# Six pairs of hidden blocks, in two groups of three, take seven products in GEMM2; a convolution's two filters come ahead of v; four row tiles load by halves

## The chip, the cores and the metric

The kernel runs on one core of a Trainium2 chip. The metric is the device time of one execution in microseconds (us). TensorE (PE) multiplies, VectorE (DVE) and ScalarE (ACT) do elementwise work, GpSimd (POOL) and SyncE (SP) issue the transfers (DMAs); each engine works through its own instructions in order.

## The reference

```
xn  = layernorm(x)                                  # x: 2048 x 1024
h   = silu(xn @ w1)                                 # w1: 1024 x 3584
ffn = h @ w2                                        # w2: 3584 x 1024
kv  = shift(k) * v                                  # 4 taps along the sequence, per channel
y   = irfft(rfft(pad kv) * rfft(pad ssm_k)) + kv * ssm_D
out = x + xn * y + ffn
```

The shapes are S = 2048 rows, D = 1024 channels and F = 3584 hidden columns, all float32.

## The kernel before, in words

**Numbers.** Every float32 operand of a matrix product is split into two float16 parts, hi and lo (`split`: ScalarE writes hi = scale x source, VectorE writes lo = the rest). A product of two operands is three matmuls: hi x hi, hi x lo, lo x hi.

**The two GEMMs.** GEMM1 makes the 28 hidden blocks of 128 columns, two by two (14 pairs), for all 16 row tiles of 128 rows. Of the 28 combinations of a pair and a half of the rows, 26 go through `units`, a seven-product (Strassen-like) form: of a 2 x 2 product of blocks it makes seven products P1 to P7 instead of eight, with sums of blocks as factors. GEMM2 multiplies the hidden blocks by w2, whose 1024 result columns fall into two halves of W = 512.

GEMM2 has two parts. The *plain* part takes the blocks that are not in `PAIRS` (`PLAIN`, 20 of 28) in `NC` = 5 chunks of four, for each half of the columns h and each row tile t: twelve matmuls per chunk (`steps2`, L1128 to L1130), summed in one PSUM bank over the chunks, and written out by `result`. The *seven-product* part (`units2`) takes the blocks of the four pairs of `PAIRS`. It has eight units; one is a 2 x 2 product of two row tiles (`tiles2`) by the two halves of the columns. A unit makes P1, P7, P6, P2, P5, P3, P4, each of twelve matmuls (four pairs x three). Products share banks: P6, P5 and P3 are added onto a copy of P1 in a second bank, so each of them waits until `evacuate2` has copied the bank's last state away (`seen`), and P4 is added onto P7's bank. Four results per unit are scaled and added to `out` in memory. The factors for this form are made beforehand: `quad` makes the seven sums of the hidden blocks during GEMM1 and stores them (`hsf`), and `norms_w2` makes the seven factors of w2 and keeps them in the eight large buffers `places`.

**The convolution.** `convolution` runs beside both GEMMs, on 8 groups g of 128 channels. Per group: `gate` (four taps and the product with v, on ScalarE and VectorE), `signal_parts` (hi and lo parts), `stage1` (matmuls of a long transform, L1630 to L1632, whose banks `to_spec` empties with ScalarE and VectorE), `transforms` (forward, spectrum product and inverse, all on VectorE), `result_parts` and `stage1_inv` (matmuls back, L1818 to L1820), `gated` (product with xn, and the write to `out`). `stage1` of group g can empty its banks only when the parts of group g - 1 are taken. It has the two PSUM banks of `ps_r`; the inverse and small norms have the two of `py_r`; the feed-forward part has four (`ff`), of which one may be lent when `spare()` says so: between GEMM1's end and the last part.

**What sets the order.** A planner on the host (`Order`) holds many streams of steps; it gives each step a cost, picks the step that can start first (with a small bias per stream) and emits it to its engine. So the order on each engine is fixed before the run, and an engine that waits holds up all behind it. `flag[...]` tokens order the streams among themselves; on the chip, semaphores follow the data.

**Writes to `out`.** Three contributions meet in each element: plain part, seven-product part, convolution. `L` is a plain transfer from SP, `G` an adding transfer from POOL. The plain part's first half of columns and the convolution's first four groups store with `L`; the others add with `G` and wait for the flags `row` or `conv row`. The very last unit waits for `conv out`, all writes of the convolution, before it goes on past P6: it then loads the tile of `out`, adds to it, and stores with `L`.

**The start.** `load_row` loads a row tile of x (128 x 1024, 512 KB) in one transfer; VectorE takes the statistics of each half of it (L546). Until the first row tiles are normalised, transposed and split, TensorE runs filler matmuls (L1896, L1903).

Of the kernel before, what the change touches and what calls it, by code (L numbers as in the profile page):

```python
# [20 lines left out]
P = 128  # L21
# [4 lines left out]
NT = S // P  # L26
# [27 lines left out]
PAIRS = (8, 9, 10, 11)  # L54
UNITS = [[*range(2, NP)], [NP - 1, 0, 1, *range(2, NP - 1)]]
NQ = len(PAIRS)
# [246 lines left out]
def h3_ffn_kernel(ctx, tc, x, kp, vs, fs, shift, dskip, w1, w2, cfwd, cinv, out):  # L303
# [77 lines left out]
    hsf = [{p[0]: dram.tile([4, P, NQ, 2, P], F16, name=f"hsf{p[0]}{b}") for p in PRODUCTS.values()} for b in range(2)]  # L381
# [474 lines left out]
    def quad(i, sp):  # L856

        def factors(names, hf, toks=()):
# [4 lines left out]
            for f, name in enumerate(names):  # L863
                yield L(hsf[sp][name][:, :, PAIRS.index(i)].rearrange("q p h s -> p q (h s)"),
                        ht[:, 4 * f:4 * f + 4].rearrange("p q h s -> p q (h s)"))
                ttok.set()
# [18 lines left out]
    for sp in range(2):  # L885
        flag["quads", sp] = Token(NQ)

# [197 lines left out]
    def feed_forward():  # L1085
# [13 lines left out]
        for h in range(2):  # L1099
            for ts in TOGETHER[h]:  # L1100
                pos = {}
                for c in range(NC):
                    for t in ts:
                        if c == 0:
                            yield ff.ready
                            pos[t] = ff.tile([P, W])
                        yield flag["h", h, t, c]
                        hx, htok = flag["h", h, t, c].what
                        yield flag["w2", h, c]
                        wc, wtok = w2c[h, c]  # L1110
                        yield from steps2(pos[t][0], hx, wc, c == 0, c == NC - 1)
                        htok.set()
                        if t == NT - 1:
                            wtok.set()
                        if c == NC - 1:
                            add(result(h, t, *pos[t]), EB)
        flag["last part"].set()
        yield from units2()


    TOGETHER = ([range(3)] + [(t,) for t in range(3, NT)],
                [(t,) for t in range(NT - 3)] + [range(NT - 3, NT)])

    def steps2(po, hx, wc, first, last, more=False):
        for n in range(4):
            def mm(n=n):
# [3 lines left out]
                nc.tensor.matmul(po, hx[:, n, 1, :], wc[:, n, 0, :], start=False, stop=last and n == 3, **kw)  # L1130
# [15 lines left out]
    def units2():  # L1146

        def product2(n, u, o, first=False, cols=slice(0, W), end=True):
            yield flag["h2", u, n]
            hx, htok = flag["h2", u, n].what  # L1150
            yield flag["w2f", n]
            wc, wtok = w2f[n]
            yield from steps2(o[:, cols], hx, wc[:, :, :, cols], first, True, not first)
# [5 lines left out]
        def start(u):  # L1159
# [4 lines left out]
            add(evacuate2(u, one, made, seen), EB)  # L1164
# [3 lines left out]
        for u in range(len(tiles2)):  # L1168
# [23 lines left out]
            if u + 1 < len(tiles2):  # L1192
                following = yield from start(u + 1)
# [4 lines left out]
            if u + 1 < len(tiles2):  # L1198
# [6 lines left out]

    def at(u, r, h):

        sp, q = tiles2[u]
        t = 4 * (2 * sp + r) + q
        return orr[t // T2, t % T2, :, h * W:(h + 1) * W]  # L1210

    def evacuate2(u, one, made, seen):

        last = u == len(tiles2) - 1
# [5 lines left out]
        def copied(src, tok, to):  # L1220
# [3 lines left out]
            yield G(to, o)  # L1224
# [16 lines left out]
        if not last:  # L1241
            yield made["P2"]
            add(copied(*one, at(u, 0, 0)), EB)
# [7 lines left out]
        if last:  # L1251
            yield made["P2"]
            add(copied(*one, at(u, 0, 0)), EB)
        yield G(at(u, 1, 1), d)
# [5 lines left out]
        add(copied(two, k2, at(u, 0, 1)), EB)  # L1260
        if not last:
# [3 lines left out]
            yield G(at(u, 1, 0), a)  # L1265
# [11 lines left out]
    for n in range(NT):  # L1277
        flag["conv row", n] = Token(NG // 2)

    def columns(h):  # L1280

        return slice((1 - h) * W, (2 - h) * W)

    def result(h, t, po, tok):
# [4 lines left out]
        to = orr[t // T2, t % T2, :, columns(h)]  # L1289
        if h == 0:  # L1290
            yield L(to, o)
            flag["row", t].set()
        else:
            yield flag["conv row", t]
            yield G(to, o)
        otok.set()

    def load_h():
        yield flag["factors"]
        for h in range(2):  # L1300
            for c, t in [(c, t) for ts in TOGETHER[h] for c in range(NC) for t in ts]:
# [4 lines left out]
        for u, n in uses2():  # L1306
            sp, q = tiles2[u]
            yield wo.ready
            flag["h2", u, n].what = o, _ = wo.tile([P, NQ, 2, P], F16)
            yield L(o, hsf[sp][PRODUCTS[n][0]][q])  # L1310
            flag["h2", u, n].set()
# [20 lines left out]
    def norms_w2():  # L1332
# [17 lines left out]
        add(load_w2(), 0.05)  # L1350
        for h in range(2):
            for c in range(NC):
                r = places[W2PLACE[h][c]]
                yield r.ready
                if (h, c) == (0, 0):
                    yield flag["x", 1, "A22"]
                wc, wtok = w2c[h, c] = r.tile([P, 4, 2, W], F16)
                flag["w2", h, c].n = 2
                for a in (0, 2):
                    i = PLAIN[4 * c + a] // 2  # L1360
                    raw, tok = yield from next_w2()
# [607 lines left out]
```

## Time and profile before

| what | value |
|---|---|
| three runs | 1238.85, 1239.23, 1240.17 us; median 1239.23 |
| the profiled execution, its own time | 1239.78 us |
| its span, first to last instruction | 1237.8 us |
| granted TensorE clock | 0.999 |
| first and last GEMM1 matmul of L985 | 15.6 and 574.8 us |
| first and last GEMM2 matmul of L1128 | 576.7 and 1232.4 us |
| first and last matmul of the transform, L1630 | 278.5 and 1135.9 us |
| data moved | 278.77 MB, 225 GB/s on the mean |

Times in the page and the views are microseconds from the span's start, unless marked ns. A row of a group of instructions reads: line, engine, operation, out<-in by the program's names, shapes, count | busy us, mean ns of one | idle time of the engine just before them, and what ended it. A row of a window reads: from:to, length, then for each engine its busy time and its instructions, the granted clock, the share of time in which the DMA engines were busy, and GB/s. A row of the timeline reads: start, duration, engine, line, operation, out<-in, count, and in brackets the idle time before it and what ended it. A row of the waits reads: who <- for whom: us in total, times, longest.

### The profile page before, as it was taken

To read this page: it belongs to the slowest core of one execution; us is meant where nothing else is said; L and a number is where in the kernel's file an instruction comes from. 1 tells how busy PE (TensorE), PEld (TensorE's weight loads), DVE (VectorE), ACT (ScalarE), POOL (GpSimd) and SP (SyncE) were. 2 spreads that over 40 slices of the span, in tenths; PEclk is the share of its full clock that TensorE was granted. 3 is DMA by queue.
4 is the path that set the end of the run, shared out by engine and by line. 5 is a ranking of instruction groups with operands and counts; after the bars stand their busy time and mean duration, and the time that the engine had idled before them with its cause. 6 is when DMAs were issued, how large, how long until landed. Compare 5 with 4: busy or idle time off the path is not lost.

```text
span 1237.8 us, 16864 instructions
## 1 busy us (share of the span) xinstructions
PE 1227.2 (99%) x6044; PEld 597.6 (48%) x6044; DVE 1106.9 (89%) x1248; ACT 775.0 (63%) x1357; POOL 83.3 (7%) x93
## 2 busy tenths in 40 slices
PE   9999999999999999999999999999999999999998
PEld 8544444444444544445444544544454454444444
DVE  7999996996999779998999899799889979997992
ACT  7868897886687877659643832734363365536243
POOL 0000000000000000000000000001030130113114
PEclk9999999999999999999999999999999999999999
DMA  9598989899799889989876556489586775877767
GB/s 368 128 315 271 318 298 327 264 255 214 252 320 293 235 270 273 312 231 321 297 245 175 154 183 172 135 280 275 129 177 169 168 162 153 190 160 128 156 134 102
DMA packets 277700, 278.77 MB, mean 225 GB/s; under 512 B 85616, under 2 KB 204656, under 8 KB 276336
## 3 DMA queue, kind: packets, MB, share of 16 engines
q1 hardware_dynamic: 261888, 261.17, 70.0%
q0 software_dynamic: 15728, 16.52, 10.3%
q8 instruction: 47, 0.77, 0.3%
q14 instruction: 37, 0.30, 0.1%
HBM read 171.46 MB, written 88.34 MB: 210 GB/s over the span
## 4 chain that ended last, share of the span: by engine, by line
PE 79%; DVE 15%; issue 3%; ACT 1%; DMA 1%; SPq 0%; DVEq 0%; ACTq 0%
PE ff L1128 13%; PE ff L1129 13%; PE ff L1130 13%; PE ff L985 9%; PE ff L986 9%; PE ff L987 9%; DVE spec L351 3%; DVE ht L354 2%; DVE x L354 2%; PE ps L1630 2%; PE ps L1631 2%; PE ps L1632 2%; DVE tmp L351 1%; DVE hf L351 1%; DVE wo L354 1%
## 5 line engine op out<-in xcount | busy, mean ns | idle before, releaser
L1128 PE MATMUL ff<-x,wo 128*128 128x512 f16 x868 | 328.1, 378 | 1.8 <-ACT hf L362 1.2
L1130 PE MATMUL ff<-x,wo 128*128 128x512 f16 x868 | 328.1, 378 | 0.0
L1129 PE MATMUL ff<-x,wo 128*128 128x512 f16 x868 | 328.1, 378 | 0.0
L985 PE MATMUL ff<-x,wo 128*128 128x512 f16 (+1 forms) x808 | 302.7, 375 | 0.5 <-DVE hf L351 0.5
L987 PE MATMUL ff<-x,wo 128*128 128x512 f16 (+1 forms) x808 | 302.8, 375 | 0.0
L986 PE MATMUL ff<-x,wo 128*128 128x512 f16 (+1 forms) x808 | 302.8, 375 | 0.0
L351 DVE TENSOR_TENSOR spec<-spec 128x1024 f32<-128x1024 f32 (+2 forms) x232 | 260.0, 1147 | 2.3
L1130 PEld LDWEIGHTS <-wo 128*128 128x128 f16 x868 | 84.9, 98 | 101.6
L1129 PEld LDWEIGHTS <-wo 128*128 128x128 f16 x868 | 84.9, 98 | 101.1 <-issue 2.3
L1128 PEld LDWEIGHTS <-wo 128*128 128x128 f16 x868 | 85.8, 99 | 99.0
L987 PEld LDWEIGHTS <-wo 128*128 128x128 f16 x808 | 79.0, 98 | 92.4 <-DVE wo L354 0.5
L985 PEld LDWEIGHTS <-wo 128*128 128x128 f16 x808 | 80.5, 100 | 88.2
L986 PEld LDWEIGHTS <-wo 128*128 128x128 f16 x808 | 79.0, 98 | 89.2 <-issue 1.0
L351 DVE TENSOR_TENSOR tmp<-spec 128x2048 f32<-128x2048 f32 (+1 forms) x48 | 92.2, 1933 | 0.8
L354 DVE SCALAR_TENSOR_TENSOR ht<-hf,wsc,ht 128x1024 f16<-128x1024 f32 (+1 forms) x56 | 67.2, 1204 | 14.0 <-ACT ht L362 14.0
L362 ACT ACTIVATE spec<-spec 128x1024 bf16<-128x1024 f32 x32 | 33.7, 1053 | 65.9 <-DVE spec L351 65.9
L354 DVE SCALAR_TENSOR_TENSOR wo<-raw,wsc,wo 128x1024 f16<-128x1024 f32 (+1 forms) x56 | 63.9, 1146 | 3.5 <-ACT wo L362 3.4
L362 ACT ACTIVATE wo<-raw,wsc 128x1024 f16<-128x1024 f32 (+1 forms) x56 | 57.7, 1033 | 11.4 <-DVE raw L351 8.7
L354 DVE SCALAR_TENSOR_TENSOR sig<-kin,taps,sig 128x1024 f32<-128x1024 f32 x48 | 61.5, 1282 | 2.4 <-ACT sig L362 2.3
L362 ACT ACTIVATE ht<-hf,wsc 128x1024 f16<-128x1024 f32 (+1 forms) x56 | 60.7, 1085 | 4.1 <-DVE hf L351 2.6
L351 DVE TENSOR_TENSOR spec<-tmp 128x512 f32<-128x512 f32 (+1 forms) x80 | 61.0, 794 | 1.0
L348 POOL DMA_DIRECT2D out<-hf x44 | 38.5, 874 | 344.6 <-ACT hf L362 217.9
(191 smaller groups left out, 1697.1 us busy)
## 6 DMA issues: line engine op xcount, KB each, us to landing
wo<-hs SPq DMA_DIRECT2D x160, 256.0 KB, 3.6
hs<-ht SPq DMA_DIRECT2D x80, 256.0 KB, 4.8
raw<-in_w SPq DMA_DIRECT2D x28, 512.0 KB, 5.7
wraw<-in_w SPq DMA_DIRECT2D x24, 512.0 KB, 5.4
w2n<-in_w SPq DMA_DIRECT2D x24, 512.0 KB, 6.1
ws_T<-wo SPq DMA_DIRECT2D x22, 512.0 KB, 5.7
kin<-in_kp SPq DMA_DIRECT2D x16, 704.0 KB, 4.8
wo<-ws_T SPq DMA_DIRECT2D x22, 512.0 KB, 4.8
```

The source lines that it names most:

```text
L348: return Op("POOL", 1.1, 3.0, lambda: nc.gpsimd.dma_start(o, i, accum_op=ADD), [i], [o], m, 2.3 * n)
L351: return V(lambda: nc.vector.tensor_tensor(o, a, b, op=op), o, [a, b], **k)
L354: return V(lambda: nc.vector.scalar_tensor_tensor(o, a, s, b, op0=op0, op1=op1), o, [a, b] + ([] if isinstance(s, float) else [s]), **k)
L362: nc.scalar.activation(o, i, func, scale=scale, **kw)
L985: nc.tensor.matmul(o, w[:, 0, k], xf[:, :, k, 0], start=first and k == 0, stop=False, **kw)
L986: nc.tensor.matmul(o, w[:, 0, k], xf[:, :, k, 1], start=False, stop=False, **kw)
L987: nc.tensor.matmul(o, w[:, 1, k], xf[:, :, k, 0], start=False, stop=last and k == KH - 1, **kw)
L1128: nc.tensor.matmul(po, hx[:, n, 0, :], wc[:, n, 0, :], start=first and n == 0, stop=False, **kw)
L1129: nc.tensor.matmul(po, hx[:, n, 0, :], wc[:, n, 1, :], start=False, stop=False, **kw)
L1130: nc.tensor.matmul(po, hx[:, n, 1, :], wc[:, n, 0, :], start=False, stop=last and n == 3, **kw)
L1630: nc.tensor.matmul(o, cf[:, 0], h, start=i == 0, stop=False, **kw)
L1631: nc.tensor.matmul(o, cf[:, 0], l, start=False, stop=False, **kw)
```

## The change

- `PAIRS` holds six pairs instead of four, as two `GROUPS` of three. The plain part takes 16 blocks in 4 chunks. GEMM2 runs: plain part of the second half of the columns, seven-product units of the first group, plain part of the first half, units of the second group. Every product of a unit has nine matmuls (three pairs x three); there are two times eight units.
- The factors of the hidden blocks are made and stored for six pairs; those of w2 are made group by group (`seven_w2`), each in the places that the parts before it give back.
- Row tiles are taken three at a time at both ends of either plain part.
- Writes: a general rule (`written`, `put`). Whoever writes a piece first stores it with `L`; everybody later waits for that store to be issued and adds with `G`. A write that meets both cases is cut in two.
- `gate`: both halves' taps come first, then both products with v.
- `bank_for`: `stage1` may use a bank of `py_r` as well, from the second group on and once the parts of the group before are taken; `spare()` lends a feed-forward bank also in the second plain part, and not while units run.
- `load_row`: the first four row tiles come as two transfers of half the columns.

```diff
-PAIRS = (8, 9, 10, 11)
+GROUPS = ((6, 7, 8), (9, 10, 11))
+PAIRS = sum(GROUPS, ())
-W2PLACE = [(2, 6, 4, 0, 3), (1, 5, 7, 2, 6)]
-FPLACE = (4, 0, 3, 1, 5, 7, 2, 6)
+W2PLACE = ((2, 6, 4, 0), (3, 5, 7, 1))
+FPLACE = ((3, 1, 5, 7, 2, 6, 4, 0), (4, 2, 0, 6, 3, 5, 7, 1))
...
-        yield L(xts[t][0], xr[t // T2, t % T2])
+        for c in range(0, D, W if t < 4 else D):
+            cols = slice(c, c + (W if t < 4 else D))
+            yield L(xts[t][0][:, cols], xr[t // T2, t % T2, :, cols])
...
-        flag["last part"].set()
-        yield from units2()
+            flag["seven", h].set()
+            yield from units2(h)
+            flag["plain", h + 1].set()
...
-    def steps2(po, hx, wc, first, last, more=False):
-        for n in range(4):
+    def steps2(po, hx, wc, first, last, more=False, count=4):
+        for n in range(count):
...
+    def written(places_in, to, o):
+
+        new = [q not in first for q in places_in]
+        assert len(set(new)) == 1
+        if new[0]:
+            for q in places_in:
+                first[q] = Token()
+            yield L(to, o)
+            for q in places_in:
+                first[q].set()
+            return
+        for q in places_in:
+            yield first[q]
+        yield G(to, o)
...
                     for j in (2, 1, 0):
                         yield v_stt(o, kin[:, HALO - j:HALO - j + T2], tap[j], o, MUL, ADD)
                     tok.set()
+                for b in range(2):
+                    o = acc[:, b]
                     yield flag["v", g, b]
                     v = sig[:, 1, b]
                     yield v_tt(o, o, v, MUL)
...
-                                yield lambda: ps_r.ready() or spare()
-                                ps, tok = (ps_r if ps_r.ready() else ff).tile([P, 2, 2 * P])
+                                yield lambda: bank_for(g, t) is not None
+                                ps, tok = bank_for(g, t).tile([P, 2, 2 * P])
...
+        def bank_for(g, t):
+
+            if ps_r.ready():
+                return ps_r
+            if g > 0 and py_r.ready() and flag["taken", g - 1, t]():
+                return py_r
+            return ff if spare() else None
+
         def spare():
-            return flag["gemm1"]() and not flag["last part"]() and len(ff.free()) > 1
+            if not flag["gemm1"]() or len(ff.free()) < 2:
+                return False
+            return not flag["seven", 0]() or flag["plain", 1]() and not flag["seven", 1]()
```

More of the change, by code (lines that the diff above doesn't have):

```diff
@@ L1276, in h3_ffn_kernel, with result @@
     flag["conv out"] = Token(NG * 4 * 2)
[L1277 to L1284, printed above, removed]
+    first = {}
+    def written(places_in, to, o):
[11 more added lines that the diff above has]
+        yield G(to, o)
+    def result(k, t, po, tok):
+        h = columns(k)
         yield vs_r.ready
```

227 lines of the change are left out of this document (120 added, 107 removed).

## The prediction

> **What bounds the kernel now.** I read the page first: busy shares, the chain that ended last, the costliest groups.
>
> ```profile
> PE 1227.2 (99%) x6044; PEld 597.6 (48%) x6044; DVE 1106.9 (89%) x1248; ACT 775.0 (63%) x1357; POOL 83.3 (7%) x93
> DVE  7999996996999779998999899799889979997992
> PE 79%; DVE 15%; issue 3%; ACT 1%; DMA 1%; SPq 0%; DVEq 0%; ACTq 0%
> L1128 PE MATMUL ff<-x,wo 128*128 128x512 f16 x868 | 328.1, 378 | 1.8 <-ACT hf L362 1.2
> ```
>
> TensorE is busy 99% of the span, so on this page the stream of matmuls sets the time. The matmuls of a group overlap in their records (378 ns each), so their real spacing is read from the timeline, and what stops them in GEMM2 from the waits:
>
> ```profile
> 1179.71 0.38 PE L1130 MATMUL ff<-x,wo 128*128 128x512 f16 x1
> ...
> 1187.48 0.38 PE L1130 MATMUL ff<-x,wo 128*128 128x512 f16 x1
> ```
>
> ```profile
> PE ff L1128 <- ACT hf L362: 1.2, 1, 1.2
> ...
> PE ff L1128 <- DVE hf L354: 0.6, 1, 0.6
> ```
>
> Between the two rows lie 36 matmuls: 7.77 / 36 = 0.2158 us each. In all of GEMM2 TensorE stands still for 1.8 us.
>
> But VectorE is busy 89% too, and the windows by stage (GEMM1, GEMM2 up to its last part, the seven-product units) show little room in it:
>
> ```profile
> core 0: us, PE busy (x) PEld busy (x) DVE busy (x) ACT busy (x) POOL busy (x), PEclk, DMA share, GB/s
> ...
> 68.00:576.50 508.50, 507.61 (x2416) 236.77 (x2415) 463.09 (x537) 394.31 (x623) 3.22 (x4) 1.00 0.93 280
> 576.50:1085.00 508.50, 508.21 (x2474) 242.26 (x2473) 467.65 (x467) 262.44 (x518) 36.43 (x38) 1.00 0.71 195
> 1085.00:1217.00 132.00, 130.77 (x657) 64.14 (x655) 112.80 (x114) 59.13 (x112) 36.44 (x39) 1.00 0.76 139
> ```
>
> VectorE idles 45.4 + 40.9 + 19.2 = 105.5 us of these 1149 us. At 1217 its last operation of the convolution ends, and the tail shows that this is just in time:
>
> ```profile
> 1220.36 1.25 POOL L348 DMA_DIRECT2D out<-ht  x1
> ```
>
> ```profile
> 1220.85 0.33 SPq L338 DMA_DIRECT2D ht<-out  x1
> ```
>
> ```profile
> 1225.76 0.69 ACT L362 ACTIVATE ht<-ff,invc 128x512 f32<-128x512 f32 x1 [5.89 <-DMA out<-ht]
> ```
>
> ```profile
> 1229.33 0.27 PE L1128 MATMUL ff<-x,wo 128*128 128x256 f16 x1
> ```
>
> The last unit may not go on before the convolution's last write is issued (1220.36). ScalarE's copy of P5 waits for that write to give back a buffer and ends at 1226.45; P3, which needs it, starts twelve matmuls before P4's first at 1229.33, that is at 1226.74. The margin is 0.3 us. So two things bound this kernel at once, the matmul stream and the convolution on VectorE.
>
> **The change: TensorE.** Before, 32 plain result tiles take 5 chunks x 12 matmuls (1920) and 8 units 7 x 12 (672). After: 32 x 4 x 12 = 1536 and 16 units x 7 x 9 = 1008. The halved last P4 is left out on both sides. That is 48 fewer, 48 x 0.2158 = 10.4 us, all in a gapless stream. A product now gives 9 matmuls of cover, 1.94 us, where it gave 2.59, for the copy that frees its bank:
>
> ```profile
> L362 ACT ACTIVATE ff<-ff 128x512 f32<-128x512 f32 x34 | 19.7, 580 | 22.4 <-PE ff L987 14.3 <-PE ff L1130 8.0
> ...
> L354 DVE SCALAR_TENSOR_TENSOR ht<-hf,wsc,ht 128x512 f16<-128x512 f32 x8 | 6.0, 748 | 0.3 <-ACT ht L362 0.3
> ...
> L354 DVE SCALAR_TENSOR_TENSOR ht<-hf,wsc,ht 128x1024 f16<-128x1024 f32 x48 | 61.3, 1280 | 13.7 <-ACT ht L362 13.7
> ...
> L351 DVE TENSOR_TENSOR hf<-ff,hf 128x512 f32<-128x512 f32 x52 | 35.7, 687 | 9.0 <-PE ff L987 7.3 <-ACT hf L362 1.6
> ...
> L354 DVE SCALAR_TENSOR_TENSOR x<-w2n,tau,x 128x1024 f16<-128x1024 f32 x10 | 12.8, 1282 | 3.3 <-ACT x L362 3.3
> ...
> L354 DVE SCALAR_TENSOR_TENSOR hf<-ff,invc,hf 128x512 f32<-128x512 f32 x14 | 10.4, 746 | 0.5 <-ACT hf L362 0.5
> ...
> L354 DVE SCALAR_TENSOR_TENSOR x<-x,tau,x 128x512 f16<-128x512 f32 x12 | 8.4, 750 | 2.2 <-ACT x L362 2.2
> ```
>
> A 0.58 us copy behind one 1.1 us activation still fits. With twice the units I double today's 1.8 us: +1.8 (0 to 8, half a microsecond at each of 16 units). If nothing else binds: 1239.2 - 10.4 + 1.8 = 1230.6. This counts differences against the profiled execution (span 1237.8, its own time 1239.78, so 2.0 lie around it) and sets them on the median, 1239.23, 0.55 below that execution.
>
> **VectorE.** The same rows price what two more pairs cost it.
> - hidden factors in GEMM1: a pair's four block splits of 1024 go; each half of the rows adds three, one of 512, and four sums of 512. For two pairs net 4 x 1.280 + 4 x 0.748 + 16 x 0.687 = 19.1.
> - weights: 4 splits of 1024 go, 14 of 512 and 8 sums come: -5.1 + 10.5 + 5.5 = 10.9.
> - units: 8 more, two operations each: 16 x 0.746 = 11.9.
>
> That is 41.9 us in 58 operations. But in a row they overlap a little:
>
> ```profile
> 1034.12 2.74 DVE L354 SCALAR_TENSOR_TENSOR x<-x,tau,x 128x512 f16<-128x512 f32 x4 [2.23 <-ACT x L362]
> ```
>
> (2.74 - 0.75) / 3 = 0.663 from start to start, 0.087 less than the mean; 58 x 0.087 = 5.0, so **36.9 us** more work. Nearly all of it lies ahead of the convolution's last operation, and the edit takes no VectorE operation out. ScalarE gets about as much and is 63% busy; it matters only in the windows below.
>
> So, with R the idle time of VectorE that the new kernel recovers, the convolution ends 36.9 - R later. After its end the last unit has two products to go, shorter by 6 x 0.2158 = 1.3. The time is 1239.2 + 36.9 - R - 0.3 - 1.3 = **1274.5 - R**, or 1230.6 if that is larger. No change needs R = 35.3, the full gain R = 43.9, out of 105.5.
>
> Where is that idle time? The windows from one group's inverse transform to the next group's first transform hold most of it:
>
> ```profile
> 278.00:316.00 38.00, 37.63 (x179) 17.45 (x178) 25.92 (x29) 23.34 (x34) 0.00 (x0) 1.00 1.07 229
> 409.00:456.00 47.00, 47.00 (x243) 23.61 (x242) 32.08 (x34) 42.99 (x79) 0.00 (x0) 1.00 0.78 238
> ...
> 776.00:804.00 28.00, 28.00 (x155) 15.06 (x154) 19.52 (x23) 24.48 (x50) 0.00 (x0) 1.00 0.47 125
> ...
> 1091.00:1138.00 47.00, 47.00 (x244) 23.81 (x243) 35.81 (x41) 27.80 (x54) 14.93 (x15) 1.00 0.77 137
> 1203.00:1217.00 14.00, 14.00 (x90) 8.65 (x89) 6.96 (x9) 10.32 (x21) 7.94 (x9) 1.00 0.73 82
> sum 273.00, PE 272.34 PEld 141.24 DVE 192.74 ACT 214.11 POOL 42.27; mean PE 30.26 PEld 15.69 DVE 21.42 ACT 23.79 POOL 4.70
> ```
>
> ```profile
> DVE tmp L351 <- ACT spec L362: 31.4, 20, 3.9
> ...
> DVE spec L351 <- ACT spec L362: 16.1, 8, 3.4
> ```
>
> The nine windows, cut by hand, idle 273.0 - 192.7 = 80.3 us; the first (12.1) and the last (7.0) left out, 61.1 in seven. VectorE waits there for ScalarE to empty the transform's banks. Two banks serve it, and a spare one of the feed-forward part during GEMM2's plain tiles: the window at 776 with a spare takes 28 us, those at 409 and 1091 without one take 47. The new bank_for lends it the two inverse-transform banks (py) in all seven, at a price: the inverse and the norms wait for a lent bank, and while the first group's units run the spare one is withheld. One bank cut the window by 40%; I take it that two more halve the idle time: 30.6. Of the 36.9 us of new work, the share that falls into the windows, 36.9 x 273 / 1149 = 8.8, runs in idle time. R = 39.4, and the time 1235.1: **1235**. Bounds: R = 8.8 (nothing but the filling, 1265.7) to 43.9 and more.
>
> **The rest.** Both filters ahead of v: the waits of VectorE name no load of v, so nothing stands to be removed; the first product with v starts one filter later (three operations of about 1.28), and the next transform, a whole group away, covers that. Cost nil, 0 to 4 us if that cover goes, per group.
>
> Writes: the first writer of a tile stores plainly, later ones add through POOL. I count some 32 more accumulating writes (79 now), and conv writes split in two in places.
>
> ```profile
> L348 POOL DMA_DIRECT2D out<-hf x44 | 38.5, 874 | 344.6 <-ACT hf L362 217.9 <-ACT csc L486 85.3 <-DVE hf L354 39.2
> ```
>
> 32 x 0.874 = 28 us on a queue that is 93% idle: hidden. Each waits for the first write to land, and behind it POOL's later writes wait and with them their buffers, as today. SP gets 46 more issues (hidden factors -16 + 28 - 32 + 56, weights 6, row tiles 4), and some 10 MB more are moved, 8 of them the added writes of 256 KB; in GEMM2 the DMA share is 0.71 to 0.76, so I cost both at nothing, up to 2 us.
>
> Row tiles by halves: four more issues ahead of the first weights.
>
> ```profile
> 0.74 0.88 SPq L338 DMA_DIRECT2D xt<-in_x  x2
> ```
>
> ```profile
> 4.55 1.29 DVE L546 BATCH_NORM_STATS2 st<-xt 128x6 f32<-128x512 f32 x2 [3.45 <-DMA xt<-in_x]
> ```
>
> An issue takes 0.44 us; VectorE waits 3.45 for the first tile, and half of it might come 0.5 earlier, while the weights' loads move back by up to 4 x 0.44. I take 0 (-0.5 to +1). The Trainium skill's Perfetto Trace Analysis, DMA Optimizations, points both ways: larger transfers use the memory better, smaller ones may let work start sooner when the engines are idle. By its first half the sum would be 1 worse, by its second 0.5 better.
>
> **Rivals.**
> *Slower: ScalarE, not the banks, sets the windows (0.30).* It is busy 43.0 of 47 us at 409 and 24.5 of 28 at 776, and the units add copies to it. Then only the window at 1091 (ScalarE 27.8 of 47) and the one at 409 come down to the 8.5 us idle of the one at 776: 2.7 + 6.4, with the filling R = 17.9, and the time is **1257**. The place is P3 of the last unit, waiting for the convolution's last write; it decides against the change wherever R stays under 35. Against it: in the long window at 1091 ScalarE had room.
> *Full gain (0.14).* R over 44: **1230.6**. For it: the chain of waits is 79% TensorE. Against it: the 0.3 us margin.
> *Even (0.14).* The lent banks do little more than make room for what was added; R = 33 to 36: **1239**, gain spent on the wait at the end.
> *POOL holds up VectorE (0.02).* 32 issues of 0.874 us taken from VectorE too are 28 us: 1235 + 28 = **1263**. The rows speak against it, one operation before and during the accumulating writes:
>
> ```profile
> L351 DVE TENSOR_TENSOR tmp<-tmp,spec x8: 1218/1225/1226, 644.0 to 758.6; 128x1024 f32<-128x1024 f32 x8
> ```
>
> ```profile
> L351 DVE TENSOR_TENSOR tmp<-tmp,spec x16: 1216/1224/1226, 850.2 to 1181.9; 128x1024 f32<-128x1024 f32 x16
> ```
>
> No operation is stretched. The Trainium skill's SBUF — State Buffer, "SBUF: two separate sides", says that VectorE and GpSimd share a port pair that one holds at a time while the other is fully blocked; if an accumulating issue takes that pair, this rival would be the likely one, and the rows do not bear it out.
>
> **How the numbers follow.** The forecast has 0.40, with its own range of 1231 to 1238 (R = 36.5 to 43.5). 0.2%, or 2.5 us, is about what a measurement of this kernel can tell from no change: faster is under 1236.7, slower over 1241.7. Of the forecast 0.36 is faster and 0.04 the same. Faster 0.36 + 0.14 = 0.50, same 0.04 + 0.14 = 0.18, slower 0.30 + 0.02 = 0.32. The range 1229 to 1256 leaves out the upper half of the slower rival (R under 18.5) and a few cases below: under 2 in 10.
>
> **What would show it.** GEMM2's two groups with 2553 matmuls at 0.216; VectorE's busy time up by about 37; idle time in the windows of groups 1 to 7 near 4 us each; the convolution's last operation near 1214 and a wait of TensorE of 4 to 5 us ahead of the last unit's P3. A wait of 20 us there, with windows as idle as now, would be the slower rival; no wait at all the full gain. I would be wrong in kind if TensorE stood still inside the units (bank copies late by more than 0.5 us each) or if VectorE's work did not grow.

## The result and the profile after

The changed kernel takes **1256.98 us** (median of 4 runs, 1256.59 to 1257.62); the kernel before, beside it, 1239.7. The ratio is 1.0141, with a 95% interval of 1.0130 to 1.0153: slower by 1.4%, where 1235 was forecast. The profiled execution has a span of 1255.3 us, 17.5 more than before. Its page, the lines that answer to those shown of before:

```profile
PE 1222.3 (97%) x5989; PEld 592.5 (47%) x5989; DVE 1145.3 (91%) x1306; ACT 809.5 (64%) x1415; POOL 113.2 (9%) x127
...
DVE  7999996997999889999999899889999989997993
...
L1131 PE MATMUL ff<-x,wo 128*128 128x512 f16 x851 | 323.0, 380 | 9.5 <-ACT hf L363 6.3
...
L992 PE MATMUL ff<-x,wo 128*128 128x512 f16 (+1 forms) x808 | 302.8, 375 | 5.2 <-DVE wo L355 5.1
L990 PE MATMUL ff<-x,wo 128*128 128x512 f16 (+1 forms) x808 | 302.8, 375 | 4.3 <-ACT wo L363 3.4
```

(Lines have moved: GEMM1's matmuls are L990 to L992 now, GEMM2's L1131 to L1133.) GEMM2 has 3 x 851 = 2553 matmuls, as forecast, and VectorE works 38.4 us more, as forecast. What is new is the last number of the matmul lines: TensorE now stands still. The waits of TensorE, who <- for whom, us in total, times, longest:

```profile
PE ff L1131 <- ACT hf L363: 6.3, 4, 5.0
PE ff L992 <- DVE wo L355: 5.1, 4, 2.2
PE ff L990 <- ACT wo L363: 3.4, 3, 2.0
...
PE ff L1131 <- DVE hf L355: 2.4, 3, 1.2
```

Before, GEMM1 lost 0.5 us and GEMM2 1.8. Now GEMM1 lacks the factors of w1 (`wo`) for 8.5 us, in seven stops between 210 and 255, and GEMM2 stands 9.5 us, 5.0 of it at once, at 902. The same three stages as before, by windows:

```profile
68.00:598.00 530.00, 519.41 (x2476) 242.06 (x2474) 491.32 (x576) 411.61 (x656) 3.22 (x4) 1.00 0.91 279
598.00:1106.00 508.00, 501.64 (x2416) 237.26 (x2415) 474.65 (x480) 273.93 (x534) 62.03 (x67) 0.99 0.79 205
1106.00:1238.50 132.50, 129.94 (x651) 63.48 (x650) 117.85 (x124) 67.28 (x125) 40.17 (x43) 1.00 0.80 147
```

VectorE idles 38.7 + 33.3 + 14.7 = 86.7 us until the convolution's last operation, 105.5 before: R = 18.8. And the tail (timeline, all engines):

```profile
1237.03 1.09 POOL L349 DMA_DIRECT2D out<-ht  x1 [0.59 <-issue]
...
1237.66 0.69 DVE L352 TENSOR_TENSOR ht<-py,ht 128x512 f32<-128x512 f32 x1 [1.26 <-ACT py L363]
...
1239.19 0.33 SPq L339 DMA_DIRECT2D ht<-out  x1
...
1242.77 0.69 ACT L363 ACTIVATE ht<-ff,invc 128x512 f32<-128x512 f32 x1 [4.53 <-DMA out<-ht]
...
1243.50 0.38 PE L1131 MATMUL ff<-x,wo 128*128 128x512 f16 x1 [0.61 <-ACT ht L363]
```

The convolution ends at 1238.4 instead of 1216.8, and the last unit's P3 still waits only 0.6 us: for ScalarE's copy at 1242.77, which waits for a buffer that the convolution's write issued at 1237.03 gives back. So both ends have moved: the convolution's by 21.6 us, TensorE's last matmul by 14.7 (1232.9 to 1247.6). TensorE's sum: 51 matmuls fewer, six of them of half width, are -10.4; the first GEMM1 matmul comes 2.6 later in this execution, of which 2.3 stay; between 205 and 310 it falls back by 10.3; in GEMM2 by 12.2 (9.5 of stops and 2.7 of slower clock after the stop at 902); together +14.4.

The other 2.8 of the span's 17.5 us lie behind the last matmul: 7.8 us follow it now, 5.0 before. SP's last two stores, before and after:

```profile
1232.01 1.73 SPq L338 DMA_DIRECT2D out<-hf  x2
```

```profile
1248.12 0.89 SPq L339 DMA_DIRECT2D out<-hf  x2
```

From issue to landing they take 5.2 us on the mean, 3.9 before. Beside them POOL's last four adding writes, issued from 1244.23 on, land until 1253.6. They may hold the stores up; no run tests it.

### The profile page after: what moved, and what is told of

It is laid out like the page before. It is cut to its first block, busy times and chain, and to the rows that moved or that the text cites. A ratio compares the mean times of both kernels' runs of the same rounds, so it can differ in the third digit from the quotient of the medians.

```text
span 1255.3 us, 17090 instructions
## 1 busy us (share of the span) xinstructions
PE 1222.3 (97%) x5989; PEld 592.5 (47%) x5989; DVE 1145.3 (91%) x1306; ACT 809.5 (64%) x1415; POOL 113.2 (9%) x127
## 4 chain that ended last, share of the span: by engine, by line
PE 73%; DVE 13%; issue 6%; DMA 3%; POOL 1%; ACT 1%; SPq 1%; DVEq 0%; POOLq 0%; ACTq 0%
PE ff L992 11%; PE ff L990 11%; PE ff L991 11%; PE ff L1131 10%; PE ff L1133 10%; PE ff L1132 10%; DVE spec L352 3%; DVE x L355 2%; DVE tmp L352 2%; PE ps L1668 2%; PE ps L1669 2%; PE ps L1670 2%; POOL out L349 1%; DVE ht L355 1%; DVE sig L355 1%
## 5 line engine op out<-in xcount | busy, mean ns | idle before, releaser
L1131 PE MATMUL ff<-x,wo 128*128 128x512 f16 x851 | 323.0, 380 | 9.5 <-ACT hf L363 6.3
L1132 PE MATMUL ff<-x,wo 128*128 128x512 f16 x851 | 322.9, 379 | 0.0
L1133 PE MATMUL ff<-x,wo 128*128 128x512 f16 x851 | 322.9, 379 | 0.0
L992 PE MATMUL ff<-x,wo 128*128 128x512 f16 (+1 forms) x808 | 302.8, 375 | 5.2 <-DVE wo L355 5.1
L990 PE MATMUL ff<-x,wo 128*128 128x512 f16 (+1 forms) x808 | 302.8, 375 | 4.3 <-ACT wo L363 3.4
L1133 PEld LDWEIGHTS <-wo 128*128 128x128 f16 x851 | 83.5, 98 | 100.6 <-issue 1.4
L1131 PEld LDWEIGHTS <-wo 128*128 128x128 f16 x851 | 84.4, 99 | 98.0 <-issue 0.8
L992 PEld LDWEIGHTS <-wo 128*128 128x128 f16 x808 | 79.0, 98 | 99.1 <-DVE wo L355 7.7
L990 PEld LDWEIGHTS <-wo 128*128 128x128 f16 x808 | 80.5, 100 | 92.2 <-ACT wo L363 4.8
L349 POOL DMA_DIRECT2D out<-hf x76 | 66.9, 904 | 326.1 <-ACT hf L363 230.9
L363 ACT ACTIVATE hf<-ff,invc 128x512 f32<-128x512 f32 x61 | 41.1, 682 | 57.9 <-PE ff L1133 47.5
L349 POOL DMA_DIRECT2D kf<-in_dskip x8 | 6.7, 832 | 760.1 <-DVE tmp L352 224.8
```

Source lines behind the costliest of these rows:

```text
L349: return Op("POOL", 1.1, 3.0, lambda: nc.gpsimd.dma_start(o, i, accum_op=ADD), [i], [o], m, 2.3 * n)
L363: nc.scalar.activation(o, i, func, scale=scale, **kw)
L990: nc.tensor.matmul(o, w[:, 0, k], xf[:, :, k, 0], start=first and k == 0, stop=False, **kw)
L992: nc.tensor.matmul(o, w[:, 1, k], xf[:, :, k, 0], start=False, stop=last and k == KH - 1, **kw)
L1131: nc.tensor.matmul(po, hx[:, n, 0, :], wc[:, n, 0, :], start=first and n == 0, stop=False, **kw)
L1132: nc.tensor.matmul(po, hx[:, n, 0, :], wc[:, n, 1, :], start=False, stop=False, **kw)
```

## Experiments: do the companions cost or earn anything?

Theory: the six pairs cost the time, by both ends. Rivals: a companion edit does (loan, gate, halves), or one end alone.

*b_bank*, the kernel before with only the loan:

```diff
-    yield lambda: ps_r.ready() or spare()
-    ps, tok = (ps_r if ps_r.ready() else ff).tile([P, 2, 2 * P])
+    yield lambda: bank_for(g, t) is not None
+    ps, tok = bank_for(g, t).tile([P, 2, 2 * P])
```

> The kernel before with the loan of the inverse transform's two banks alone. Theory (two ends bind the kernel before, 0.3 us apart): VectorE idles 10 to 20 us less and the convolution ends 5 to 18 us earlier than 1216.8, but TensorE's stream, 99% busy, does not get shorter, so the time is 1236 to 1240, the same within 0.2% or at best 2 us faster. If the convolution's end alone set the time of the kernel before: 1222 to 1232.

*b_rest*, with the gate's order and the row halves as well:

> The kernel before with the loan, the gate's new order and the row tiles by halves, that is the change without the six pairs and without the new rule of the writes. If the six pairs carry the whole loss: 1236 to 1240, as for the loan alone. If one of the companions costs something by itself (row halves at the head, 0 to 2.5 us; the gate's order): 1241 to 1245.

Measured: 1240.11 and 1239.58 beside 1240.21, ratios 1.0004 (0.9995 to 1.0012) and 0.9996 (0.9984 to 1.0009). The convolution's last operation in b_bank:

```profile
1206.15 0.69 DVE L351 TENSOR_TENSOR ht<-py,ht 128x512 f32<-128x512 f32 x1 [1.91 <-ACT py L362]
```

It ends 10.0 us earlier than before (in b_rest 13.1), and the time does not move: TensorE's stream holds it. So these companions by themselves are worth nothing. The loss comes with the six pairs and what goes with them (the order of GEMM2's parts, the row tiles by threes, the rule for the writes), which no run takes apart.

In the changed kernel each was taken back. *a_nobank* (the loan undone):

> The changed kernel without the loan of the inverse transform's two banks (the transform empties its banks as before, with two of its own and a spare one of the feed-forward part). The prediction's term (the loan halves the idle time of seven windows, 30 us): without it VectorE idles 20 us or more in addition and the time is 1270 to 1285. Theory A (ScalarE, not the banks, sets most windows): the idle time rises by 3 to 9 us, the time is 1258 to 1266. Nothing from the loan at all: 1255 to 1258.

Measured 1267.76, ratio 1.0229 (1.0210 to 1.0247); the convolution ends here:

```profile
1252.26 0.69 DVE L352 TENSOR_TENSOR ht<-py,ht 128x512 f32<-128x512 f32 x1 [1.79 <-ACT py L363]
```

That is 14.6 us later than with the loan. VectorE idles 104.2 us to there, as much as before the change: the loan is worth 17.5 us of idle time here, and the new work by itself has filled 1.3. Taken in the other order the shares differ: in b_bank, from 68 to the convolution's end, VectorE idles 95.7 us, so there the loan is worth 9.8 of the 105.5, and the step from there to the changed kernel fills 9.0.

*a_nogate* (filter, product, filter, product):

> The changed kernel with the old order in the gate: filter, product with v, filter, product with v. The prediction priced the new order at nothing (0 to 4 us per group). If the second filter's three operations, put ahead in the stretch 215 to 245 where VectorE is busy all the time, are what makes the factors of w1 late: TensorE's delay at 310 falls by 4 to 8, and the time is 1249 to 1254. If not: 1255.5 to 1258.5.

Measured 1260.87, ratio 1.0180 (1.0163 to 1.0197): the new order helps by about 4 us, it does not starve GEMM1.

*a_nohalves*:

```diff
-        for c in range(0, D, W if t < 4 else D):
-            cols = slice(c, c + (W if t < 4 else D))
-            yield L(xts[t][0][:, cols], xr[t // T2, t % T2, :, cols])
+        yield L(xts[t][0], xr[t // T2, t % T2])
```

> The changed kernel with the first four row tiles loaded whole again. In the changed kernel TensorE stands still for 2.50 us ahead of the first transposes, and its first GEMM1 matmul starts at 18.2 us instead of 15.6. If the halves are the cause, the first matmul is back near 15.6 and the time falls by 2.3, to about 1254.6. If the end of the kernel is set by the convolution on VectorE alone, the first matmul comes earlier but the time falls by less than 1.

Measured 1257.81, ratio 1.0143 (1.0128 to 1.0159): no difference. The first GEMM1 matmul is at 15.7 here, and the 2.5 us won there are lost again by 310, while the granted clock between 200 and 320 is 0.96, where the changed kernel's profiled execution had 1.00.

## Experiments: which end sets the time?

*a_7g* and *b_7g* leave the convolution's last group out of the changed kernel and of the kernel before:

```diff
-for g in range(NG):
+for g in range(NG - 1):
```

> The changed kernel without the eighth group of the convolution (its 128 channels get no convolution term): some 85 us less work on VectorE and 96 transform matmuls less on TensorE, about 15.6 us. To be read against the kernel before without the same group. Theory A (VectorE's work sets the end): relieved of the group, the changed kernel is no longer slower than the kernel before; the difference is between -10 and +4 us. Theory B (separate stalls that have nothing to do with the load on VectorE): the difference stays at +17.

> The kernel before without the eighth group of the convolution (its 128 channels get no convolution term). Its matmul stream is without gaps, so both theories expect it at 1239 less 15.6 us of transform matmuls, about 1223.6.

Measured: 1236.9 (ratio 0.9979, 0.9967 to 0.9990) and 1224.48 (0.9885, 0.9868 to 0.9901). The kernel before loses 15 us with the group, the changed one 20; with no convolution near its end the change still costs 12.4. So the convolution's end isn't the only cause, and the stop at 902 was looked at. The first reading was a load of w2 (issued at 895.18), with a split that waits for it ahead of the bank copy on ScalarE. *a_w2late* was to test it:

```diff
+    def LL(o, i):
+        op = L(o, i)
+        op.late = 8.0
+        return op
...
-                yield L(raw, w2r[:, j:j + 2, half * W:(half + 1) * W])
+                yield LL(raw, w2r[:, j:j + 2, half * W:(half + 1) * W])
```

> The changed kernel, with the planner told that a load of w2 lands 8 us after its issue (it took 9 us at 895), so that on ScalarE the split which waits for it is put behind the copies of the unit's bank. No work is taken away. Theory B (the single stop of 5.0 us at 902 and the lower clock of the ten microseconds behind it are paid in full): the stop goes, TensorE's delay against the kernel before does not rise by 8 to 10 near 900, and the time is 1247 to 1251. Theory A (VectorE's work sets the end): the stop goes, but the convolution's last operation stays within 3 us of 1238, TensorE waits that much longer ahead of the last unit's P3, and the time is 1254 to 1258.

Measured 1260.05, ratio 1.0166 (1.0151 to 1.0181), and the stop is still there, 4.8 us at 907. But the edit did not move what it was to move: the split (`x<-wraw`), and a second one, still stand ahead of the copy (`hf<-ff`) on ScalarE of a_w2late:

```profile
908.90 1.13 ACT L368 ACTIVATE x<-wraw,tau 128x1024 f16<-128x1024 f32 x1
...
910.13 1.13 ACT L368 ACTIVATE x<-w2n,tau 128x1024 f16<-128x1024 f32 x1
...
911.36 1.24 ACT L368 ACTIVATE hf<-ff,invc 128x512 f32<-128x512 f32 x2
```

So this run does not decide. The timeline of the changed kernel at 902 does; by engine (ScalarE, then VectorE, then TensorE):

```profile
901.74 0.27 ACT L363 ACTIVATE pow<-py,tiny 128x4 f32<-128x4 f32 x1 [3.00 <-PE py L499]
...
904.42 0.20 ACT L488 ACTIVATE csc<-pow 128x1 f32<-128x1 f32 x1 [2.33 <-DVE pow L505]
904.53 1.13 ACT L363 ACTIVATE x<-wraw,tau 128x1024 f16<-128x1024 f32 x1
...
905.99 0.67 ACT L363 ACTIVATE hf<-ff,invc 128x512 f32<-128x512 f32 x1
```

```profile
901.65 2.48 DVE L352 TENSOR_TENSOR spec<-spec 128x1024 f32<-128x1024 f32 x2
904.04 0.15 DVE L503 TENSOR_SCALAR pow<-pow 128x1 int32<-128x1 int32 x1
```

```profile
906.71 0.59 PE L1131 MATMUL ff<-x,wo 128*128 128x512 f16 x1 [5.01 <-ACT hf L363]
907.09 0.63 PE L1132 MATMUL ff<-x,wo 128*128 128x512 f16 x1
907.52 0.63 PE L1133 MATMUL ff<-x,wo 128*128 128x512 f16 x1
```

The split of w2 (904.53) waits for nothing of its own, so it is not a late load. The bank copy (`hf<-ff` at 905.99) stands on ScalarE behind a scale of the convolution (`csc`), which waits 2.33 us for tiny operations of VectorE (`pow`, 0.15 us each) that are queued behind two of its 1.2 us ones; the split, 1.13 us, comes between. ScalarE isn't short of time: it keeps its order. The units of the first group copy their P1 from 786 to 896, in the midst of convolution groups, where before the change the first such copy came at 1068. *a_copyfirst* puts the copies ahead:

```diff
+    EU = 0.2
...
-            add(evacuate2(k, u, one, made, seen), EB)
+            add(evacuate2(k, u, one, made, seen), EU)
...
-        add(copied(two, k2, row_of(u, 0), 1), EB)
+        add(copied(two, k2, row_of(u, 0), 1), EU)
```

> The changed kernel with the priority of the units' bank copies in GEMM2 raised (bias 0.06 to 0.2), so that ScalarE's copy at 902 stands ahead of the convolution's scale (which waits for VectorE) and of two splits of w2. No work is taken away. Theory B (that single stop of TensorE, 5.0 us and the slower clock behind it, is paid in full): the stop goes and the time falls to 1246 to 1250. Theory A (the convolution's end sets the time as well, so what is saved there is waited for at the end): the stop goes, but TensorE stands 5 to 10 us ahead of the last unit's last products, and the time is 1254 to 1262.

*a_7g_copyfirst* is the same without the last group:

> The changed kernel with the units' copies first and without the last of the eight groups of the convolution (its 128 channels are left out), beside 1236.9 for the changed kernel without that group. With that group gone nothing waits for the convolution at the end. If the stop at 902 is paid in full once the convolution's end does not bind: 1227 to 1231. If the stop is paid back elsewhere: 1234 to 1238.

Measured: 1258.0, ratio 1.0152 (1.0135 to 1.0169), and 1230.72, ratio 0.9928 (0.9913 to 0.9942). Waits of TensorE in a_copyfirst:

```profile
PE ff L1132 <- ACT ht L363: 4.5, 1, 4.5
PE py L1867 <- DVE ht L352: 3.6, 1, 3.6
```

The stop at 902 is gone and two others have come, at 1229 and 1238, 8.1 us, both for the convolution's last group, which ends at 1240.2. Four numbers tell it: taking the stop away is worth nothing with the whole convolution (1257.0 to 1258.0), and 6.2 us without its last group (1236.9 to 1230.7). Two ends bind at once, and what one is given goes to the wait for the other.

## Experiments: where do the stops in GEMM1 come from?

TensorE in two windows, of before and of the changed kernel:

```profile
200.00:230.00 30.00, 30.00 (x144) 13.94 (x142) 26.38 (x35) 26.77 (x45) 0.00 (x0) 1.00 0.81 268
230.00:260.00 30.00, 30.00 (x142) 13.57 (x141) 29.76 (x36) 24.89 (x39) 0.00 (x0) 1.00 0.91 286
```

```profile
200.00:230.00 30.00, 25.08 (x118) 10.99 (x117) 22.14 (x29) 22.73 (x37) 0.94 (x1) 1.00 0.92 308
230.00:260.00 30.00, 26.30 (x122) 11.55 (x121) 29.69 (x37) 24.76 (x41) 0.00 (x0) 1.00 0.83 269
```

No engine is fuller than before; TensorE lacks 8.6 us. The order of SP's transfers tells more, before and after:

```profile
195.43 1.87 SPq L338 DMA_DIRECT2D raw<-in_w  x2
```

```profile
196.29 7.46 SPq L339 DMA_DIRECT2D hsfS<-ht  x4
203.84 2.33 SPq L339 DMA_DIRECT2D ws_T<-wo  x1
206.27 0.38 SPq L339 DMA_DIRECT2D ws_B<-wo  x1
206.74 0.68 SPq L339 DMA_DIRECT2D raw<-in_w  x1
```

The same load of w1 is issued 11.3 us later, behind four stores of hidden factors. Pairs 6 and 7 now have such factors, so the stores of hidden factors begin at 165 instead of 200, and those of their sums (`hsfS`) at 174 instead of 210, where w1's factors are still being made. *a_halfstores* halves them:

```diff
-    yield L(hsf[sp, k][name][:, :, a].rearrange("q p h s -> p q (h s)"),
-            ht[:, 4 * f:4 * f + 4].rearrange("p q h s -> p q (h s)"))
+    yield L(hsf[sp, k][name][:2, :, a].rearrange("q p h s -> p q (h s)"),
+            ht[:, 4 * f:4 * f + 2].rearrange("p q h s -> p q (h s)"))
...
-                yield L(o[:, :len(GROUPS[h])], hsf[sp, h][PRODUCTS[n][0]][q])
+                yield L(o[:, :len(GROUPS[h])], hsf[sp, h][PRODUCTS[n][0]][q % 2])
```

> The changed kernel that stores only two of the four row tiles of each of the hidden factors (128 KB less in each of 84 stores, 11 MB in all), and in GEMM2 loads those two again in place of the other two, so that half of the seven-product results are of the wrong rows. No engine's work changes. If the stores, which stand ahead of w1's loads in the transfers at 196 to 207, make w1's factors late: the stops of TensorE between 205 and 262 shrink from 8.5 to under 5 us and its delay at 310 from 13 to 4 to 9; the time is 1247 to 1252 if stops are paid in full, 1253 to 1257 if the convolution's end sets it. If transfers play no part: delay at 310 of 12 to 14 as before.

*a_nosums* leaves VectorE's sums out instead:

```diff
-        yield v_tt(v, z, v, ADD)
-        yield v_tt(z, x, z, SUB)
...
-        yield v_tt(x, v, x, SUB)
...
-        yield v_tt(y, y, x, SUB)
```

> The changed kernel without the 48 sums of hidden blocks (0.687 us each, some 29 us of VectorE's work in GEMM1 from start to start); the factors S1 to S4 are then plain blocks, so the seven products are not those of the reference. If VectorE's amount of work were the only thing behind the result: the stops of TensorE between 205 and 262 vanish, the convolution ends near 1212, and the time is 1230 to 1238. If the stops come from elsewhere (late loads of w1, the order on ScalarE at 902): the convolution ends earlier, but at least 5 us of stops stay in GEMM1 and the one near 902 stays, and the time is 1246 to 1252.

*a_light* does both and puts the copies first:

> The changed kernel with three things at once: without the 48 sums of hidden blocks, with half of the hidden factors' stores (so the seven-product results are not those of the reference), and with the units' copies first. If VectorE's work, the transfers ahead of w1's loads and the order on ScalarE are the causes: TensorE's delay at 310 is under 4, the stops in GEMM2 sum to under 5 us, and the time is 1234 to 1243. If removing them only brings out other waits (VectorE idle instead of busy, the convolution held by the order of its own steps): 1243 to 1250.

Counting GEMM1's groups of three, the 433rd starts at 309.1 before. It comes 12.6 us later in the changed kernel (2.3 of it from the head), 4.4 with half the stores, 7.9 without the sums, 4.1 with both (about 1 from the head in these three). The one row that a_halfstores has for the factors of w1, where the changed kernel has two, of 5.1 and 3.4 us (the load above is issued at 201.9 there):

```profile
PE ff L992 <- DVE wo L355: 1.8, 2, 1.0
```

So the stops in GEMM1 are mostly the stores' (10.3 us down to 3.5), and the sums have a part in them, which is larger than 7.9 makes it look: of that, some 1.7 us are a slower clock (granted 0.83 between 210 and 220 in a_nosums, 1.00 in the changed kernel). The times: a_halfstores 1254.79 (ratio 1.0124, 1.0108 to 1.0139), with 5.4 us of wait for the convolution at 1235; a_nosums 1247.59 (1.0065, 1.0050 to 1.0080); a_light 1250.51 (1.0087, 1.0073 to 1.0101), outside the 1234 to 1243 of the causes, and just above the 1243 to 1250 of the other case: even then stops came up elsewhere in GEMM2 (12 us between 780 and 1125), and the convolution ended at 1231.0.

## Experiments: what does the convolution's end pay for?

In a_nosums 28 us less work of VectorE brought the convolution's end only 8.5 us forward:

```profile
1229.13 0.69 DVE L352 TENSOR_TENSOR ht<-py,ht 128x512 f32<-128x512 f32 x1 [1.26 <-ACT py L363]
```

The other 20 became idle time (107.4 us to there, against 86.7). The starts of the transforms (the first matmul of `stage1`) say where the end is made. The fourth group's begins at 663.0 in b_bank, 673.4 in the changed kernel, 664.5 in a_nosums; from there to the end it takes 543.8, 564.9 and 565.3 us. So 10.4 us of the end's delay are made ahead of that point and 21.1 behind it (13.7 and 21.0 against b_rest, which has the gate's order and the halves too). The first part isn't the price of VectorE's new work in GEMM1 (19.1) alone: a_halfstores keeps all of that work, begins the fourth group's transform at 665.0 and ends the convolution at 1232.1, 6.2 us earlier, so the stores that hold up TensorE hold up the convolution too. The second part is as much as the new work of weights and units there (22.8, or 19.8 in a row). *a_now2* takes work out of that stretch, *a_now2_copyfirst* with the copies first too:

```diff
-            yield v_tt(hold[:, a], hold[:, a], b11, ADD)
...
-            yield v_tt(b21, b21, hold[:, a], SUB)
...
-            yield v_tt(hold[:, a], b22, hold[:, a], SUB)
```

> The changed kernel without 18 of the 24 sums of w2's factors (0.6 us each from start to start on VectorE, 11 us, all in GEMM2); the seven products are then not those of the reference. If VectorE's work in GEMM2 is paid in full at the convolution's end: it comes 9 to 12 us earlier, near 1228. If it is paid as the sums in GEMM1 were, a third: near 1235. The time: TensorE's own stops (902 among them) still hold it, so 1250 to 1256 in both cases.

> The same, with the units' copies first, so that the stop at 902 is gone; beside 1258.0 with the copies first alone, where the convolution's end at 1240 held the last unit. If VectorE's work in GEMM2 is paid in full: convolution's end near 1229, no wait ahead of the last products, time 1247 to 1251. If a third: end near 1236, time 1253 to 1256. Neither (a third cause): above 1256.

Measured: 1252.59 (ratio 1.0104, 1.0086 to 1.0122) and 1249.42 (1.0080, 1.0064 to 1.0096). The end in the second:

```profile
1230.09 0.69 DVE L352 TENSOR_TENSOR ht<-py,ht 128x512 f32<-128x512 f32 x1 [1.27 <-ACT py L363]
```

1230.8 against 1240.2 with the copies first alone, and in a_now2 1228.1 against 1238.4: 9.4 and 10.3 us of the 11 taken out. In GEMM2 VectorE's work is paid nearly in full. The convolution's end is thus booked as 1216.8, less 10.0 for the loan, plus 10.4 ahead of the fourth group's transform and 21.1 behind it; this adds up by construction, and a_halfstores and a_now2 are what tests its parts.

With both ends forward, a third one shows. In a_now2_copyfirst the last matmul ends at 1239.2, 6.4 us later than before the change, but 9.9 us follow it (5.0 before the change): the last adding write, issued at 1239.5, lands at 1247.2. No run takes these writes away.

## Experiments: two that misfired

*a_quadlow* gave the hidden factors' work a low priority:

```diff
-            add(quad(i, sp), 0.1)
+            add(quad(i, sp), 0.02)
...
```

> The changed kernel with one thing else: the streams that make the hidden factors of the six pairs have the bias 0.02 instead of 0.1, so that the w1 factors go first on VectorE and ScalarE. The waits of TensorE for w1 factors between 205 and 262 us (8.5 us, about 10.7 of delay) should go. Theory A (VectorE's work for the whole kernel sets the convolution's end, and the waits on the way only show it early): the time stays within 4 us of 1257 and the wait turns up later, most of it ahead of the last unit's P3. Theory B (the waits are separate costs that add up): the time falls by 8 to 11, to about 1247.

Measured 1516.52: the factors then hold the few buffers of hidden blocks so long that GEMM1 itself stands still (TensorE waits 66 us for `hf` of VectorE alone). It shows that this work can't be put off so far, not what it costs.

*a_pool* gave the sums to GpSimd:

```diff
+    def g_tt(o, a, b, op):
+        return Op("POOL", 1.5, 0.3, lambda: nc.gpsimd.tensor_tensor(o, a, b, op=op), [a, b], [o], 0.2)
...
-        yield v_tt(v, z, v, ADD)
+        yield g_tt(v, z, v, ADD)
...
```

> The changed kernel with the four sums per pair and half of the rows (48 of 512 columns in all, 0.687 us each on VectorE, some 29 us) moved from VectorE to GpSimd. Theory A (VectorE's amount of work is what binds: the convolution ends late and, in GEMM1, the factors of w1 come late because VectorE is busy all the time): the convolution's last operation moves from 1238 to 1210-1216, the stops of TensorE between 205 and 262 (11 us late by 310) shrink to under 4, and the time is 1232 to 1242. Theory B (the stops are set by the order on ScalarE and by transfers, not by VectorE's amount of work): TensorE is still 10 or more late at 310, and the time is 1248 to 1257. Rival C (GpSimd's operations hold VectorE up): VectorE's operations beside the sums are stretched by 10% or more, and the time is 1250 or over.

Measured 1295.21, ratio 1.0452 (1.0436 to 1.0468): rival C. GpSimd's sums last 1.9 us, and VectorE is held up beside them. GpSimd, then VectorE at the same time:

```profile
226.34 2.13 POOL L355 TENSOR_TENSOR x<-hf,x 128x512 f32<-128x512 f32 x1
228.55 2.13 POOL L355 TENSOR_TENSOR x<-x 128x512 f32<-128x512 f32 x1
```

```profile
227.27 2.28 DVE L358 SCALAR_TENSOR_TENSOR sig<-kin,taps,sig 128x1024 f32<-128x1024 f32 x1
229.48 2.29 DVE L358 SCALAR_TENSOR_TENSOR wo<-raw,wsc,wo 128x1024 f16<-128x1024 f32 x1
231.69 1.27 DVE L358 SCALAR_TENSOR_TENSOR sig<-kin,taps,sig 128x1024 f32<-128x1024 f32 x1
```

The same operation takes 2.28 us beside a sum and 1.27 right after the last one. In all, VectorE is busy 1152.6 us, 35.7 more than in a_nosums, which has the same operations on VectorE.

No version with six pairs came below the kernel before with the same groups of the convolution.

## Why the prediction was wrong

- *Fewer matmuls, -10.4.* Right: 2553.
- *VectorE, +36.9.* Right: +38.4.
- *The formula 1274.5 - R.* With the measured R of 18.8 it gives 1255.7, near the result, but partly by luck. The convolution's end moved by 21.6, where 36.9 - R is 18.1. P3 starts 5.1 us after that end, 4.8 less than before, where the formula has 0.3 less. From P3 to the span's end it takes 0.8 more, where the formula has 1.3 less.
- ***R = 39.4: the step that failed.*** Its main term, the loan, was too large: it was to halve the idle time of seven windows, 30.6 us, and recovers 17.5 in the changed kernel and 9.8 in the kernel before. VectorE's two waits for ScalarE to empty the transform's banks were 47.5 us before the change (31.4 and 16.1). Without the loan and with it the changed kernel has:

```profile
DVE tmp L352 <- ACT spec L363: 17.3, 13, 3.0
DVE spec L352 <- ACT spec L363: 15.0, 7, 3.3
```

```profile
DVE tmp L352 <- ACT spec L363: 13.3, 13, 2.9
DVE spec L352 <- ACT spec L363: 11.7, 8, 3.3
DVE zl L355 <- ACT zh L363: 11.4, 10, 2.3
```

  So of these waits the loan takes 7.3 us here, and 6.7 in b_bank (40.8 left). One window of 28 us beside two of 47 was no measure of what a bank is worth. Other waits for ScalarE grow: that for `zl` is 4.8 before, 9.9 with the loan alone and 11.4 here. Why ScalarE comes late there stays open; the units' copies are not needed for it. The other term, 8.8 us of new work in idle time, can't be judged: it comes out at 1.3 or 9.0, by the order in which the two are taken (above).
- *"Or 1230.6 if that is larger": failed too.* With the convolution's last group gone the change still costs 12.4 us (a_7g against b_7g), where the prediction had -8.6 for TensorE alone. So with a right R of 39.4 the time would have been about 1252 (1239.2 + 12.4, an estimate), not 1235.
- *The rival of 1257* (R = 17.9, chance 0.30) had nearly the right R and the right time; the time is in part luck, as with the formula. That ScalarE's share of the windows is the reason was only argued. Its sign in the profile, 20 us of waiting ahead of the last P3, did not show (0.6), because TensorE had become as late by itself.
- *+1.8 for the shorter cover, 0 to 8.* Wrong in place. With the copies first, the units' own small stops sum to about 4 us, inside the bounds; the single stop of 5.0 and its slower clock, from the order on ScalarE, was not in the sum. "Wrong in kind if TensorE stood still inside the units" came true at one place.
- *DMA at nothing, up to 2.* Wrong. I looked at GEMM2, where the share is 0.71 to 0.76; the stores fall into GEMM1, at 0.93, ahead of w1's loads, and cost 7 of the 10 us there.
- *Gate order nil, row halves nil, adding writes hidden.* Halves: right. Gate: about 4 us better in the changed kernel. Writes: POOL's busy time rose by 29.9 us against 28; no wait of TensorE names them apart from the convolution's at P3, but they may be behind the 2.8 us after the last matmul.

## What to carry to other kernels

When two ends lie 0.3 us apart, a gain on one is worth nothing until the other moves too: price the added work on each end, stage by stage, and count idle time as recoverable only where the wait that makes it goes away. Idle shares of an engine with a fixed order are not sure room; how much of the new work they took is open here, and work taken out of GEMM1 turned two thirds into idle time. Ask of each added transfer and each small chained operation what stands behind it in its queue: a 0.15 us operation of VectorE held ScalarE for 2.3 us, and with a split of 1.1 us behind it a bank copy, for which TensorE stood 5 us.

## What the runs showed of the hardware

GpSimd's elementwise sums stretch VectorE's operations, by 1.0 us each above; VectorE's sums `hf<-ff,hf`, which read one operand from a matmul bank, stay at 0.68 beside them. The adding transfers, which POOL issues too, stretched nothing in the kernel before. The Trainium skill's SBUF — State Buffer, "SBUF: two separate sides", says that an operation of VectorE with two inputs in SBUF contends with one of GpSimd that reads SBUF; the trace agrees, in the operations that are stretched and in those that are not.

After the stop of 5.0 us at 902 thirteen matmuls start 0.42 us apart on the mean (906.71 to 912.21) instead of 0.216, 2.7 us lost; the granted clock is 0.77 between 900 and 910. In a_7g_copyfirst stops of 2.3 and 0.6 us at 209 had the same effect (0.43 us apart from 213 on; granted clock 0.83 between 210 and 220), while 2.0 and 0.6 us at 211 in the changed kernel had none (1.00).
